# One joint transpose of the row maxima for two heads, first scores moved behind the products with v, routing in the small bank

## The chip, the cores and the metric

The kernel runs on one core of a Trainium2 chip. The metric is the device time of the whole kernel in microseconds (us). Before the change the median of three runs was 418.72 us (418.63 to 418.77). The profile comes from one more execution, which took 418.81 us.

The engines carry the names of the profile: PE multiplies matrices (PEld loads their weights), DVE is VectorE, ACT is ScalarE, POOL is GpSimd, SP issues most of the DMAs.

## What is computed

Causal attention for 8 batches of 12 heads (448 positions, 64 channels), then a soft mixture of 8 experts over all 3584 tokens, with 32 slots:

```
scores = scale * q @ k.T;  scores = where(mask, -1e9, scores)
attn = exp(scores - max(scores, -1)); attn /= sum(attn, -1) + 1e-9
x = heads side by side of attn @ v                  # 3584 x 768
logits = x @ phi                                    # 3584 x 32
d = exp(logits - logits.max(0)); d /= d.sum(0)+1e-9 # over tokens
slot_out[e] = relu((d.T @ x)[e] @ w1[e]) @ w2[e]
c = exp(logits - logits.max(1)); c /= c.sum(1)+1e-9 # over slots
return c @ slot_out
```

## The kernel before

**Pairs of heads.** The 96 heads are 48 pairs; block(p) (L507) works on pair p, with heads a = 2p and a+1. One batch is six pairs, so p % 6 says where in its batch a block stands. Every engine has an in-order queue, and a recording layer (`_InOrder`, L55) keeps the instructions in the order in which the code writes them: each queue's order is the code's order, and every row of the profile has line L65. There is no scheduler.

**Scores in two parts.** The scores of head i lie in one of three PSUM buffers, `s_[i % 3]` (each two banks of 512 columns), as blocks of keys by queries: four blocks of 128 keys with 448, 320, 192 and 64 queries. `scores1` (L249), the first scores, writes the causal mask by two bf16 matmuls (parts c03 and c12; `tri`, `identb` in the profile) and then four products k3 to k0 of rounded k and q (`s<-qd,ks`; the lower half of ks holds what rounding took from k). `max_keys` (L279) has DVE reduce this buffer by transposing 32 x 32 blocks (step 0, the large one) and folds the result by two small reductions (steps 1 and 2) into 14 columns of a tile `r`. `max_row` (L300) has PE transpose r into a small PSUM bank (`rt`) and DVE reduce it to the negated maxima `mr`. `max_spread` (L311) has POOL spread mr over rows of `r2`, next to the rest of q (`sub_q`, L243). `scores2` (L322), the second scores, adds with four matmuls both the maxima and the product with the rest of q to the buffer (`s<-r,k`). `exps` (L333) is one ACT instruction over the 1024 columns of the buffer, into `pt`.

**Products with v.** `attv` and `attv3` (L337, L351) multiply pt with v (`po<-va,pt`): 24 records for the three full query blocks of a head, and 16 for the last query block of both heads. `norm` (L368) divides by the sums, in three steps on DVE, into x. `xtrans` and `xcopy` (L386, L392) transpose x by four matmuls (`xm<-ident,x`) and copy it by ACT (`xts`).

**Routing.** `logits_a` multiplies two pairs of transposed x with phi, `logits_t` adds the result to `lt` on DVE, `logits_b` takes its maximum (`bm`, `run_m`), `logits_d` and `logits_e` make the weights of the tokens (`gs`) and transpose them and lt, `dispatch_a` multiplies them with x, and `dispatch_b` adds to `si` on DVE. Which of these a block has depends on p % 6: 1 the logits and the maximum, 2 the weights, 3 logits and a first piece of the dispatch, 4 and 0 further pieces, 5 logits. Up to p = 6 there are only logits. In the old kernel they write into the score buffer `s_[(a + 1) % 3]`, which is free at the block's end.

**PSUM.** Three score buffers (six banks), one bank po, and one small bank that `misc` (L210) hands out in turn, to rt, xm and the like: the next user waits until the last one has been read.

**Order of a block before.** PE: scores2(a), scores1(a+2), scores2(a+1), scores1(a+3), 24 products of a, rt of a+2, 24 products of a+1, 16 products, rt of a+3, the routing, xtrans(p-1). POOL: the rests of q and k for the next pairs (2 large subtractions), and two spreads, each behind its own rt. ACT: exps(a), xcopy(p-2), exps(a+1), then `copy_k2`, `cast_q` and `cast_k` for the next pairs. SP's loads of q and k stand behind the subtractions that free their buffers.

**Start and end.** Ahead of block 0 the first heads are loaded and cast by halves, and `warm` (L213) issues matmuls whose result nobody reads, START = (8, 4) of them. After block 47 come the last head's products, the last routing, the experts and the combination with the output; the change leaves that code alone.

Of the kernel before, what the change touches and what calls it, by code (L numbers as in the profile page):

```python
# [17 lines left out]
P = 128  # L18
# [7 lines left out]
NCH = 4  # L26
# [12 lines left out]
START = (8, 4)  # L39
# [9 lines left out]
RW, RC, RF = 96, 4, 20  # L49
# [31 lines left out]
def attention_soft_moe(ctx: ExitStack, tc: tile.TileContext, qk, va, phi, w1, w2, out):  # L81
# [24 lines left out]
    r_ = [fix.tile([P, RW], F32, name=f"r{i}") for i in range(2)]  # L106
# [14 lines left out]
    def load_qk(p, a, hs=slice(0, 2)):  # L121
        if p < NPAIR:
            if hs.start == 0:

                st["raw", a, p] = (wres.tile([P, 2 * WN], F32, tag="w", name=f"qk{a}_{p}")[:, 0:2 * S]
                                   .rearrange("p (h s) -> p h s", h=2)
                                   if (p, a) in ((1, 0), (2, 1)) else
                                   raw.tile([P, 2, S], F32, tag="qk", name=f"qk{a}_{p}"))
            nc.sync.dma_start(out=st["raw", a, p][:, hs], in_=qk[p, :, a, hs])
# [46 lines left out]
    load_qk(1, 1)  # L176
    load_qk(1, 0)
    loads_v(0)
    load_qk(2, 1)
    load_qk(2, 0)  # L180
    load_qk(3, 1)


# [10 lines left out]

    pob = ps_1.tile([P, 512], F32, name="po")
# [6 lines left out]
    nc.scalar.activation(out=identb, in_=ident, func=AF.Copy)  # L202
    for i in range(NR):
        nc.gpsimd.memset(r2_[i][0:64, :, :].bitcast(F32), 0.0)
        nc.vector.memset(ks_[i][:, 2 * S:2 * S + KP].bitcast(F32), 0.0)
        nc.vector.memset(r_[i], -3.0e38)
# [42 lines left out]
    def scores1(i, part):  # L249
        if i >= NHD:  # L250
            return
        p, h = divmod(i, 2)
        ks, qd = ks_[p % NR], qd_[p % NR]
        if ("s", i) not in st:
            st["s", i] = s_[i % 3]
            st["open"] = set()
        s = st["s", i]

        bank = part in ("c12", "k1", "k2")
        start = bank not in st["open"]  # L260
        st["open"].add(bank)
        if part[0] == "k":
            c = int(part[1])
            o, w, m = S * h + P * c, S - CQ0[c], min(P, S - P * c + (KP if i else 0))
            nc.tensor.matmul(s[0:m, SCOL[c]:SCOL[c] + w], ks[:, o:o + m],
                             qd[:, h, CQ0[c]:S], start=start, stop=False, skip_group_check=True)
            return
        if part == "c12":
            o = s[:, SC1:SC1 + 2 * SC2].rearrange("p (a n) -> p a n", n=SC2)[:, :, 0:P]
            mask = tri.unsqueeze(1).to_broadcast([P, 2, P])  # L270
        else:
            o, mask = s[:, SC3:SC3 + AW + P], tri2
        nc.tensor.matmul(o, identb, mask, start=start, stop=False, skip_group_check=True)

    def scores1_all(i):
        for part in ("c03", "c12", "k3", "k2", "k1", "k0"):
            scores1(i, part)

    def max_keys(i, k):  # L279

        if i >= NHD:
            return
        r = r_[i % 2]
        if k == 0:
            nc.vector.tensor_reduce(out=r[:, RC:RC + 72].rearrange("p (a b)->p a b", b=36)[:, :, 0:16],
                                    in_=st["s", i].rearrange("p (a b k)->p a b k", a=2, k=32),
                                    axis=AX.X, op=ALU.max, apply_transpose=True)  # L290
        elif k == 1:
            w = r[:, 0:84].rearrange("p (j q)->p q j", j=2)[:, 0:16]
            nc.vector.tensor_reduce(out=r[:, RF:RF + 76].rearrange("p (a q)->p a q", a=2)[:, :, 0:8],
                                    in_=w.rearrange("p (a q) j->p a q j", a=2), axis=AX.X, op=ALU.max)
        else:
            nc.vector.tensor_reduce(out=r[:, RF + 8:RF + NQB],
                                    in_=r[:, 14:80].rearrange("p (j q)->p q j", j=3)[:, 0:6],
                                    axis=AX.X, op=ALU.max)

    def max_row(i, k, w=RW - RF, to=None):  # L300
        if i >= NHD:
            return
        if k == 0:
            st["rt", i] = misc(f"rt{i}") if to is None else to
            nc.tensor.transpose(out=st["rt", i][0:w, 0:P], in_=r_[i % 2][:, RF:RF + w], identity=ident)
        else:
            mr = st["mr", i] = wk.tile([NQB, 32], F32, tag="mr", name=f"mr{i}", bufs=2)
            nc.vector.tensor_reduce(out=mr, in_=st.pop(("rt", i))[0:NQB, 0:P].rearrange("p (g t)->p t g", g=4),
                                    axis=AX.X, op=ALU.max, negate=True)

    def max_spread(i):  # L311
        if i >= NHD:
            return
        p, h = divmod(i, 2)
        mr = st.pop(("mr", i))

        nc.gpsimd.affine_select(out=r2_[p % NR][0:NQB, h].rearrange("p (b t)->p b t", t=32),
                                in_=mr.unsqueeze(1).to_broadcast([NQB, NQB, 32]),
                                compare_op=ALU.is_equal, fill=0.0, base=0,
                                pattern=[[-1, NQB], [0, 32]], channel_multiplier=1)  # L320

    def scores2(i, cs):  # L322
        if i >= NHD:
            return
        p, h = divmod(i, 2)
        s = st["s", i]
        k2, r2 = k2_, r2_[p % NR]
        for c in cs:
            o, w, m = S * h + P * c, S - CQ0[c], min(P, S - P * c + (KP if i else 0))
            nc.tensor.matmul(s[0:m, SCOL[c]:SCOL[c] + w], k2[:, o:o + m],  # L330
                             r2[:, h, CQ0[c]:S], start=False, stop=True, skip_group_check=True)
# [54 lines left out]
    def xtrans(p):  # L386
        x, xm = st.pop(("x", p)), misc(f"xm{p}")
        st["xm", p] = xm
        for c in range(NCH):
            nc.tensor.transpose(out=xm[:, P * c:P * c + P], in_=x[:, c], identity=ident)  # L390
# [58 lines left out]
    def next_logits(b, j, m):  # L449
        logits_a(b, (j, j + 1), m[:, 0:P])  # L450
        logits_t(j, m[:, 0:P])

# [32 lines left out]
    warm(START[1])  # L485
# [5 lines left out]
    nc.gpsimd.memset(si, 0.0)  # L491
    max_row(0, 0)
    max_row(0, 1)
    max_spread(0)
    scores1_all(1)
# [4 lines left out]
    sub_k(1, h1)  # L500
    for k in range(3):
        max_keys(1, k)
    sub_q(0, h1, nc.vector)
# [3 lines left out]
    def block(p):  # L507
# [10 lines left out]
        if p:  # L518
            norm(p - 1, 2)
        scores2(a, range(NCH))  # L520
        exps(a)
        if p == 0:
            copy_k2(0, h1)
            cast_q(1, h1)
        elif p > 1:
            xcopy(p - 2)
        scores1_all(a + 2)
        if p == 0:
            max_row(1, 0)
            max_row(1, 1)  # L530
            max_spread(1)
        for k in range(3):
            max_keys(a + 2, k)
        if p == 0:
            cast_k(2, h0)
# [6 lines left out]
        sub_q(p + 1)  # L542
        load_qk(p + 3, 0)
        if p:
            sub_k(p + 2)
            load_qk(p + 4, 1)
        if m6 == 2 and p > 6:
            logits_d(b, lt)
# [4 lines left out]
        if last:  # L553
            next_logits(p // 6, 2, s_[(a + 2) % 3])
# [12 lines left out]
        for h in range(2):  # L567
            attv(a + h, [(qc, 3 * h + qc, FULL) for qc in range(3)], po2, begun)
            if h == 0:
                max_row(a + 2, 0, AW)  # L570
        max_row(a + 2, 1)
        max_spread(a + 2)
        for k in (1, 2):
            max_keys(a + 3, k)
        if p == 0:
            sub_k(2, eng=nc.vector)
            load_qk(4, 1)
# [7 lines left out]
        m = s_[(a + 1) % 3]  # L585
        parts = []
        if m6 in (1, 3, 5) and p > 1:
            j = (m6 + 3) % 6
            logits_a(b if m6 == 1 else p // 6, (j, j + 1), m[:, 0:P])
        elif m6 == 2 and p > 6:  # L590
            logits_e(b, m)
        if m6 == 3 and p > 6:
            parts = [(b, 0, slice(0, P), 512)]
        elif m6 == 4 and p > 6:
            parts = [(b, 0, slice(P, 3 * P), 512)]
            if p == NPAIR - 2:
                parts += [(b, 1, slice(0, 3 * P), 0)]
        elif m6 == 0 and p > 6:
            parts = [(b - 1, 1, slice(0, 3 * P), 0)]
        for d, hf, sl, o in parts:  # L600
            dispatch_a(d, hf, m[:, o:o + sl.stop - sl.start], sl)
        if m6 in (1, 3, 5) and p > 1:
            logits_t(j, m[:, 0:P])
            if m6 == 1:
                logits_b(b, lt)
        for d, hf, sl, o in parts:
            dispatch_b(d, hf, m[:, o:o + sl.stop - sl.start], sl)
        if p:
            xtrans(p - 1)
# [319 lines left out]
```

## Time and profile before

| | value |
|---|---|
| median of three runs | 418.72 us (418.63 to 418.77) |
| profiled execution | 418.81 us, span 417.1 us, 14076 instructions |
| exponentials (pt<-s) | 96 of 1030 ns |
| large reductions on DVE (r<-s) | 96 of 1245 ns |
| transposes of maxima (rt<-ident,r) | 96 of 298 ns |
| first scores, masks included | 576 matmuls; second scores 384 |
| exponentials of head 2, and of head 94 | begin at 21.32 us and at 315.53 us |

A row of a group or of the timeline names the engine, the operation, the tiles as output<-inputs (numbers of buffers left out), shapes and a count. Starts of matmuls are recorded and their ends modelled, and matmuls overlap; so the time that PE spends on a piece of work is read here from one start to the next start. A bracket such as [1.07 <-PE s L65] tells how long the engine was idle before the instruction and what ended that. One loop turn takes about 6.4 us; the loop ends near 320 us and the experts follow.

### The profile page before, as it was taken

What the parts mean: (1) busy time and instruction counts of PE and PEld (TensorE: products, weight loads), DVE (VectorE), ACT (ScalarE), POOL (GpSimd) and SP (SyncE); (2) the same over time, 40 slices, a digit from 0 to 9 for tenths busy, and PEclk for the clock granted to TensorE, in tenths of its full rate; (3) what the DMA queues carried; (4) which work ended last, traced back from release to release, by engine and by line L of the source; (5) the groups of instructions that cost most, each with busy time, mean ns of one, the idle gap of its engine ahead of it and who ended that gap; (6) DMA issues with size and microseconds to landing.
All of it is one profiled execution on the core that took longest, in us unless ns stands there. A gap on an engine that the chain in (4) does not pass through costs nothing.

```text
span 417.1 us, 14076 instructions
## 1 busy us (share of the span) xinstructions
PE 383.6 (92%) x5710; PEld 300.0 (72%) x5710; DVE 295.2 (71%) x827; ACT 283.0 (68%) x402; POOL 263.3 (63%) x212
## 2 busy tenths in 40 slices
PE   7799999999999999999999999999998998997840
PEld 3678888888887888888888878888886644633420
DVE  6687777878877878888788778788884576433540
ACT  5677878877978888788779788887863111432430
POOL 6498898888888888988888888889862000000000
PEclk9699999999999999999999999999999999999975
DMA  7578787788777787677887777877849999999997
GB/s 275 183 228 263 251 261 224 256 260 270 236 232 243 254 283 242 224 257 247 261 270 238 230 242 255 291 236 245 278 156 415 405 426 427 421 417 415 397 394 319
DMA packets 34479, 119.16 MB, mean 286 GB/s; under 512 B 3824, under 2 KB 8944, under 8 KB 32880
## 3 DMA queue, kind: packets, MB, share of 16 engines
q1 hardware_dynamic: 34272, 118.01, 80.3%
q8 instruction: 45, 0.74, 0.7%
q10 hardware_dynamic: 144, 0.27, 0.2%
q14 instruction: 18, 0.15, 0.1%
HBM read 107.25 MB, written 11.01 MB: 284 GB/s over the span
## 4 chain that ended last, share of the span: by engine, by line
PE 78%; DVE 7%; DMA 5%; issue 3%; ACT 2%; POOL 1%; SPq 0%; DVEq 0%; POOLq 0%
PE s L65 34%; PE po L65 25%; PE xm L65 7%; PE rt L65 5%; DMA w<-in_w_dram 4%; PE so L65 2%; PE hp L65 2%; PE pp L65 2%; DVE lm L65 2%; DMA qk<-in_qk_dram 2%; DVE lg L65 1%; PE cp L65 1%; DVE r L65 1%; PE e L65 1%; DVE mr L65 1%
## 5 line engine op out<-in xcount | busy, mean ns | idle before, releaser
L65 ACT ACTIVATE pt<-s 128x1024 f32<-128x1024 f32 x96 | 98.8, 1030 | 53.5 <-PE s L65 49.9
L65 DVE TRANSPOSE_TENSOR_REDUCE r<-s 128x32 f32<-128x1024 f32 x96 | 119.5, 1245 | 20.9 <-PE s L65 18.4
L65 PE MATMUL po<-va,pt 128*64 128x65 f32 x3040 | 111.1, 226 | 0.0
L65 PEld LDWEIGHTS po<-va,pt 128*64 128x64 f32 x3040 | 97.8, 139 | 17.9 <-issue 11.9
L65 POOL TENSOR_TENSOR r<-qk,qd 64x896 fp32r<-64x896 f32 (+1 forms) x48 | 100.4, 2092 | 4.7 <-ACT qd L65 0.9
L65 POOL TENSOR_TENSOR ks<-qk,ks 64x896 fp32r<-64x896 f32 (+1 forms) x48 | 97.9, 2041 | 0.8 <-ACT ks L65 0.8
L65 POOL TENSOR_SCALAR_AFFINE_SELECT r<-mr 14x448 fp32r<-14x448 f32 x96 | 61.6, 642 | 46.2 <-DVE sm L65 26.6
L65 PE MATMUL s<-qd,ks 128*128 128x448 f32 (+4 forms) x384 | 79.8, 331 | 1.5 <-POOL ks L65 1.5
L65 PE MATMUL s<-r,k 128*128 128x448 f32 (+3 forms) x384 | 65.0, 292 | 1.4 <-POOL r L65 1.4
L65 PEld LDWEIGHTS s<-r,k 128*128 128x128 f32 (+1 forms) x384 | 59.6, 177 | 4.5 <-POOL r L65 2.3
L65 PEld LDWEIGHTS s<-qd,ks 128*128 128x128 f32 (+2 forms) x384 | 51.0, 180 | 1.7 <-POOL ks L65 1.7
L65 ACT ACTIVATE ks<-qk 128x896 fp32r<-128x896 f32 (+1 forms) x51 | 45.4, 892 | 3.7 <-DMA qk<-in_qk_dram 3.7
L65 ACT ACTIVATE qd<-qk 128x896 fp32r<-128x896 f32 (+1 forms) x50 | 46.1, 922 | 1.3
L65 ACT ACTIVATE k<-ks 64x896 fp32r<-64x896 f32 (+1 forms) x49 | 45.7, 934 | 1.1
L65 DVE TENSOR_REDUCE mr<-rt 14x32 f32<-14x128 f32 x96 | 24.8, 258 | 30.3 <-PE rt L65 30.3
L65 DVE TENSOR_REDUCE r<-r 128x16 f32<-128x32 f32 x192 | 33.7, 175 | 5.0
L65 PE MATMUL s<-tri,identb 128*128 128x192 bf16 x192 | 35.0, 264 | 0.0
L65 PE MATMUL xm<-ident,x 128*128 128x128 f32 x188 | 30.8, 286 | 3.4 <-DVE mr L65 3.4
L65 PEld LDWEIGHTS xm<-ident,x 128*128 128x128 f32 x188 | 19.7, 140 | 17.2 <-DVE sm L65 11.2
L65 PE MATMUL rt<-ident,r 128*64 128x128 f32 (+1 forms) x96 | 28.6, 298 | 1.7 <-DVE r L65 1.5
L65 ACT ACTIVATE xts<-xm 128x512 f32<-128x512 f32 x47 | 27.8, 592 | 0.2 <-PE xm L65 0.2
L65 DVE TENSOR_TENSOR x<-po,sm 128x384 f32<-128x384 f32 (+2 forms) x49 | 26.4, 540 | 0.4
(138 smaller groups left out, 355.8 us busy)
## 6 DMA issues: line engine op xcount, KB each, us to landing
qk<-in_qk_dram SPq DMA_DIRECT2D x94, 448.0 KB, 4.2
w<-in_w_dram SPq DMA_DIRECT2D x43, 768.0 KB, 7.2
w<-in_w_dram SPq DMA_DIRECT2D x10, 1536.0 KB, 20.1
va<-in_va_dram SPq DMA_DIRECT2D x47, 260.0 KB, 4.5
out_dram<-ot SPq DMA_DIRECT2D x16, 384.0 KB, 6.7
out_dram<-ot SPq DMA_DIRECT2D x2, 1536.0 KB, 9.2
qk<-in_qk_dram SPq DMA_DIRECT2D x4, 224.0 KB, 3.3
hw<-in_w_dram SPq DMA_DIRECT2D x1, 768.0 KB, 7.5
```

The costliest lines, as they stand in the source:

```text
L65: return self._tc.keep_in_program_order(op(*args, **kwargs))
```

## The change

**Maxima.** Both heads of a pair now write their folded maxima into one tile `r`, head a's from column 0 and head a+1's from column 32. One transpose `rt` per pair turns 64 columns, one DVE reduction makes mr with 46 rows, and two spreads follow each other on POOL, the second from rows 32 to 45.

**Order on PE.** scores1(a+2) stands at the head of the block, directly behind the last 16 products of the block before. Then two x transposes of pair p-2, scores2(a), two more, scores2(a+1), scores1(a+3), the routing, 24 products of a, 24 of a+1, rt of the next pair, and the 16 products.

**Routing.** It writes into the small bank amid the block. DVE's part of it comes between the large reduction of a+3 and the two small ones; ACT's copies of `logits_e` come behind exps(a+1) and ahead of `copy_k2`, and `logits_d` ahead of exps(a).

**Norm.** All three steps of the division stand at the head of the next block.

**First scores.** The parts are issued as c03, k3, c12, k2, k1, k0 instead of c03, c12, k3, k2, k1, k0; two blocks of keys of the first heads are two columns narrower.

**Start.** START = (8, 2, 2, 3), with the warming matmuls writing into po. One load of k goes through ACT's queue, loads of q and k change places, the subtractions of pairs 1 and 2 are cut by heads and partly put on DVE, and the zeroing of si moves from POOL's start to block 4.

On PE in the middle of block 15 (heads 30 and 31), before. The s_ names are the three score buffers; s_85 holds head 30 and later head 33, s_87 gets head 32, s_86 holds head 31; `r_90,k_97` or `r_98,k_97` mark second scores, `qd,ks` first scores, `tri` the mask. The four second scores of head 30 into s_85 and the first mask matmul of head 32 have just been issued:

```order
L65 MATMUL s_87<-tri_129,identb 128x2x128
L65 MATMUL s_87<-qd_88,ks_89 66x64
L65 MATMUL s_87<-qd_88,ks_89 128x192
L65 MATMUL s_87<-qd_88,ks_89 128x320
L65 MATMUL s_87<-qd_88,ks_89 128x448
L65 MATMUL s_86<-r_98,k_97 128x448
L65 MATMUL s_86<-r_98,k_97 128x320
L65 MATMUL s_86<-r_98,k_97 128x192
L65 MATMUL s_86<-r_98,k_97 66x64
L65 LDWEIGHTS identb
L65 MATMUL s_85<-tri_129,identb 128x192
```

The same place after the change, from the second scores of head 30:

```order
L65 MATMUL s_85<-r_97,k_96 128x448
L65 MATMUL s_85<-r_97,k_96 128x320
L65 MATMUL s_85<-r_97,k_96 128x192
L65 MATMUL s_85<-r_97,k_96 66x64
L65 MATMUL xm_1673<-ident,x_94 128x128 x2
L65 MATMUL s_86<-r_97,k_96 128x448
L65 MATMUL s_86<-r_97,k_96 128x320
L65 MATMUL s_86<-r_97,k_96 128x192
L65 MATMUL s_86<-r_97,k_96 66x64
L65 LDWEIGHTS identb
L65 MATMUL s_85<-tri_117,identb 128x192
```

Between the last second score of s_85 and the mask that starts head 33 in s_85 there were six matmuls of head 32 and four of head 31; now there are two x transposes and the four of head 31.

On PE at the end of block 15, before: behind the second rt follow two pairs' logits, a dispatch piece, the x transposes and the second scores of the next block.

```order
L65 MATMUL rt_1796<-ident,r_96 64x128
L65 MATMUL s_86<-xts_1622,phi_153 32x128 x4
L65 MATMUL s_86<-xts_1725,phi_153 32x128 x4
L65 MATMUL s_86<-x_103,gs 32x128 x4
L65 MATMUL xm_1818<-ident,x_94 128x128 x4
L65 MATMUL s_87<-r_90,k_97 128x448
```

After the change, from the last first score of head 33 to the only rt of the block (twelve of these matmuls with v are 24 records of the trace):

```order
L65 MATMUL s_85<-qd_88,ks_89 128x448
L65 MATMUL m_1706<-xts_1587,phi_151 32x128 x4
L65 MATMUL m_1706<-xts_1683,phi_151 32x128 x4
L65 MATMUL m_1706<-x_102,gs 32x128 x4
L65 MATMUL po<-va_99,pt_98 64x65 x12
L65 MATMUL po<-va_99,pt_100 64x65 x12
L65 MATMUL rt_1750<-ident,r 64x128
```

The routing has moved ahead of the products with v, into the bank `m`, and rt stands once, behind both heads' 24 products.

On DVE at the end of block 13 (p % 6 = 1), before: the large reduction of the second head, then its small ones, each mr behind its rt, and the routing (lt, bm, run_m) last.

```order
L65 TENSOR_REDUCE r_96<-s_87 128x2x16
L65 TENSOR_REDUCE mr_1575<-rt_1561 14x32
L65 TENSOR_REDUCE r_96<-r_96 128x2x8
L65 TENSOR_REDUCE r_96<-r_96 128x6
L65 TENSOR_REDUCE mr_1590<-rt_1588 14x32
L65 TENSOR_SCALAR sm_1593<-po 128x7
L65 RECIPROCAL sm_1593<-sm_1593 128x7
L65 TENSOR_TENSOR lt<-s_85,lt 128x128
L65 TENSOR_REDUCE bm_1605<-lt 128x1
L65 TENSOR_SCALAR run_m_156<-run_m_155,bm_1605 128x1
```

And after:

```order
L65 TENSOR_REDUCE r<-s_87 128x2x16
L65 TENSOR_TENSOR lt<-m_1504,lt 128x128
L65 TENSOR_REDUCE bm_1514<-lt 128x1
L65 TENSOR_SCALAR run_m_154<-run_m_153,bm_1514 128x1
L65 TENSOR_REDUCE r<-r 128x2x8
L65 TENSOR_REDUCE r<-r 128x6
L65 TENSOR_REDUCE mr_1548<-rt_1546 46x32
L65 TENSOR_SCALAR sm_1571<-po 128x7
```

The three routing instructions now stand ahead of the two small reductions on which rt waits.

The diff, cut to its core:

```diff
-START = (8, 4)
+START = (8, 2, 2, 3)
...
-    r_ = [fix.tile([P, RW], F32, name=f"r{i}") for i in range(2)]
+    r_ = fix.tile([P, RW], F32, name="r")
...
     def scores1_all(i):
-        for part in ("c03", "c12", "k3", "k2", "k1", "k0"):
+        for part in ("c03", "k3", "c12", "k2", "k1", "k0"):
...
-    def max_row(i, k, w=RW - RF, to=None):
-        if i >= NHD:
+    def max_row(p, k):
+        if p >= NPAIR:
             return
         if k == 0:
-            st["rt", i] = misc(f"rt{i}") if to is None else to
-            nc.tensor.transpose(out=st["rt", i][0:w, 0:P], in_=r_[i % 2][:, RF:RF + w], identity=ident)
+            st["rt", p] = misc(f"rt{p}")
+            nc.tensor.transpose(out=st["rt", p][0:AW, 0:P], in_=r_[:, 0:AW], identity=ident)
...
-        if p:
-            norm(p - 1, 2)
-        scores2(a, range(NCH))
-        exps(a)
+        if m6 == 2 and p > 6:
+            logits_d(b, lt)
         if p == 0:
...
-        elif p > 1:
-            xcopy(p - 2)
-        scores1_all(a + 2)
...
+        else:
+            scores1_all(a + 2)
+            for k in range(3):
+                norm(p - 1, k)
+            if p > 1:
+                xtrans(p - 2, range(2))
+            scores2(a, range(NCH))
+            exps(a)
+            if p > 1:
+                xtrans(p - 2, range(2, NCH))
+                xcopy(p - 2)
         for k in range(3):
             max_keys(a + 2, k)
+        if p == 4:
+            nc.gpsimd.memset(si, 0.0)
         scores2(a + 1, range(NCH))
         exps(a + 1)
...
         scores1_all(a + 3)
         max_keys(a + 3, 0)
...
+        parts = []
         if m6 == 2 and p > 6:
-            logits_d(b, lt)
+            logits_e(b, misc(f"le{p}"))
+        elif m6 in (1, 3, 5) and p > 1 or m6 in (0, 4) and p > 6:
+            m, j = misc(f"m{p}"), (m6 + 3) % 6
...
+            for d, hf, c0, c1, o in parts:
+                dispatch_a(d, hf, m[:, o:o + c1 - c0], slice(c0, c1))
+            if m6 % 2:
+                logits_t(j, m[:, 0:P])
+                if m6 == 1:
+                    logits_b(b, lt)
+            for d, hf, c0, c1, o in parts:
+                dispatch_b(d, hf, m[:, o:o + c1 - c0], slice(c0, c1))
+        for k in (1, 2):
+            max_keys(a + 3, k)
         copy_k2(p + 1)
...
         for h in range(2):
             attv(a + h, [(qc, 3 * h + qc, FULL) for qc in range(3)], po2, begun)
-            if h == 0:
-                max_row(a + 2, 0, AW)
-        max_row(a + 2, 1)
-        max_spread(a + 2)
-        for k in (1, 2):
-            max_keys(a + 3, k)
+        max_row(p + 1, 0)
+        max_row(p + 1, 1)
+        for h in range(2):
+            max_spread(p + 1, h)
...
         attv3(p)
-        max_row(a + 3, 0, AW)
-        max_row(a + 3, 1)
-        max_spread(a + 3)
-        for k in range(2):
-            norm(p, k)
...
-        if p:
-            xtrans(p - 1)
```

More of the change, by code (lines that the diff above doesn't have):

```diff
@@ L313, in max_spread @@
             return
[L314 to L318, printed above, removed]
+        mr, r = st["mr", p], slice(32 * h, 32 * h + NQB)
+        nc.gpsimd.affine_select(out=r2_[p % NR][r, h].rearrange("p (b t)->p b t", t=32),
+                                in_=mr[r].unsqueeze(1).to_broadcast([NQB, NQB, 32]),
                                 compare_op=ALU.is_equal, fill=0.0, base=0,
@@ L384, in norm, with xtrans @@
                                         scalar1=sm[a:a + AW, 2 * m:2 * m + 1], scalar2=None, op0=ALU.mult)
[L386 to L389, printed above, removed]
+    def xtrans(p, cs=range(NCH)):
+        if cs[0] == 0:
+            st["xm", p] = misc(f"xm{p}")
+        x, xm = st["x", p], st["xm", p]
+        for c in cs:
             nc.tensor.transpose(out=xm[:, P * c:P * c + P], in_=x[:, c], identity=ident)
@@ L568, in block @@
             attv(a + h, [(qc, 3 * h + qc, FULL) for qc in range(3)], po2, begun)
-            if h == 0:
-                max_row(a + 2, 0, AW)
-        max_row(a + 2, 1)
-        max_spread(a + 2)
-        for k in (1, 2):
-            max_keys(a + 3, k)
+        max_row(p + 1, 0)
+        max_row(p + 1, 1)
+        for h in range(2):
+            max_spread(p + 1, h)
         if p == 0:
-            sub_k(2, eng=nc.vector)
-            load_qk(4, 1)
+            sub_k(2, h1)
         attv3(p)
-        max_row(a + 3, 0, AW)
-        max_row(a + 3, 1)
-        max_spread(a + 3)
-        for k in range(2):
-            norm(p, k)
[L585 to L607, printed above, removed]
-        if p:
-            xtrans(p - 1)
     for p in range(NPAIR):
```

95 lines of the change are left out of this document (53 added, 42 removed).

## The prediction

> **What bounds it.** I read first the busy times (of the page, and of a long stretch of the loop over pairs), then the chain piece by piece, then the timeline of one block. The first says which engine is short, the second what a block costs, the third what is waited for within it.
>
> ```profile
> PE 383.6 (92%) x5710; PEld 300.0 (72%) x5710; DVE 295.2 (71%) x827; ACT 283.0 (68%) x402; POOL 263.3 (63%) x212
> 60.00:300.00 240.00, 238.36 (x3868) 202.03 (x3867) 194.48 (x539) 201.58 (x266) 205.70 (x151) 1.00 0.77 252
> ```
>
> The second row gives PE, PEld, DVE, ACT and POOL in turn, for 240 us of the loop, some 38 blocks. PE has holes of 1.6 us in all; POOL, ACT and DVE have 34, 38 and 46 us, so 0.9 to 1.2 us in each block. Whatever PE issues here is paid for, and so is whatever makes it stand.
>
> ```profile
> 103.97 2.52 PE s L65 x20
> ...
> 110.22 2.58 PE s L65 x20
> ...
> 116.81 2.52 PE s L65 x20
> 119.33 0.85 PE po L65 x24
> 120.17 0.23 PE rt L65
> 120.41 1.32 PE po L65 x40
> 121.72 0.23 PE rt L65
> 121.95 0.57 PE s L65 x8
> 122.52 0.59 PE xm L65 x4
> 123.11 2.51 PE s L65 x20
> ...
> 129.40 2.52 PE s L65 x20
> ...
> 135.91 2.51 PE s L65 x20
> ...
> 142.21 2.52 PE s L65 x20
> ```
>
> These are pieces of the chain (start, us, what). A block reads: twenty score matmuls, products with v of head a (po x24), a transpose of maxima (rt), the other products (po x40), the second rt, a routing piece (the short "s"), the x transposes (xm). From one "x20" to the next are the periods of blocks 14 to 19, one batch of six: 6.25, 6.59, 6.30, 6.29, 6.51, 6.30, together 38.24 us.
>
> **The window that decides.** Block 17 in the timeline:
>
> ```profile
> 122.45 0.66 PE L65 MATMUL xm<-ident,x 128*128 128x128 f32 x4
> 122.86 0.71 PE L65 MATMUL s<-r,k 128*128 128x448 f32 x4
> 123.42 0.36 PE L65 MATMUL s<-tri,identb 128*128 128x192 bf16 x2
> 123.61 1.03 ACT L65 ACTIVATE pt<-s 128x1024 f32<-128x1024 f32 x1 [1.07 <-PE s L65]
> 124.19 0.63 PE L65 MATMUL s<-r,k 128*128 128x448 f32 x4
> 124.39 1.25 DVE L65 TRANSPOSE_TENSOR_REDUCE r<-s 128x32 f32<-128x1024 f32 x1 [0.30 <-PE s L65]
> 124.69 0.35 PE L65 MATMUL s<-tri,identb 128*128 128x192 bf16 x2
> 124.80 0.82 PE L65 MATMUL s<-qd,ks 128*66 128x64 f32 x4
> 125.55 0.86 PE L65 MATMUL po<-va,pt 128*64 128x65 f32 x22
> 125.68 0.40 DVE L65 TENSOR_REDUCE r<-r 128x16 f32<-128x32 f32 x2
> ```
>
> By starts: second scores of a at 122.86, first scores of a+2 at 123.42 (0.56 later), second scores of a+1 at 124.19 (0.77), first scores of a+3 at 124.69 (0.50), products with v at 125.55 (0.86). There are three score buffers, so head a+3 writes the one that held head a. Its first matmul must wait for the exponentials of head a: these run from 123.61 to 124.64, and it starts at 124.69. So 1.83 us lie between the second scores of a and the first scores of a+3 whatever PE does between, and the old order has just that much to do there: 0.56 + 0.77 + 0.50.
>
> **The change in the loop.** It takes the first scores of a+2 (0.77) out of this window and puts them ahead of it. In their place comes half of the x transposes; all four take 122.86 − 122.45 = 0.41, so half 0.20. PE reaches head a+3 after 0.56 + 0.20 + 0.50 = 1.26 and stands for 1.83 − 1.26 = 0.57 us. Behind it are queued the scores, the routing and all products with v, and DVE's maxima wait for those scores. The exponentials cannot start earlier, since ACT already waits for PE there (idle 1.07). One of the two transposes of maxima goes (0.23).
>
> A new block by starts: first scores 0.77, half of x 0.20, window 1.83, first scores 0.86, routing M, 48 products 0.85 + 24/40 × 1.32 = 1.64, a wait W for the maxima, rt 0.23, the last 16 products 0.53. That is 6.06 + M + W. The old one was 2.69 + 0.85 + 0.23 + 1.32 + 0.23 + 0.41 = 5.73 + M. So each block gains **0.33 + W**. M is the old period less 5.73, thus 0.57 in blocks 16, 17, 19, 0.86 in block 15, 0.78 in block 18. Block 14 is other: it has only two transposes as routing (0.20, as above), and its old period hides a wait of the x transposes for the small bank, 0.3; the new order ends that.
>
> W is there because the one rt now needs the maxima of both heads. I count from the second scores of a. The first scores of a+3 end at 124.80 + 0.82, so at 2.76. The large reduction follows 0.03 later, as at 124.39; with its 1.25 and the two small ones rt may start at 4.51. PE gets there at 1.83 + 0.86 + 1.64 = 4.33 + M. But DVE's part of the routing now stands between the large reduction and the small ones:
>
> ```profile
> L65 DVE SCALAR_TENSOR_TENSOR si<-si,al,s 128x384 f32<-128x384 f32 x7 | 4.3, 614 | 1.3 <-PE s L65 1.3
> L65 DVE TENSOR_TENSOR lt<-s,lt 128x128 f32<-128x128 f32 x14 | 4.1, 292 | 1.3 <-PE s L65 1.1
> L65 DVE SCALAR_TENSOR_TENSOR si<-si,al,s 128x256 f32<-128x256 f32 x7 | 3.4, 481 | 0.7 <-PE s L65 0.7
> L65 DVE SCALAR_TENSOR_TENSOR si<-si,al,s 128x128 f32<-128x128 f32 x7 | 2.4, 339 | 0.0
> L65 DVE TENSOR_REDUCE bm<-lt 128x1 f32<-128x128 f32 x7 | 2.0, 286 | 0.2
> L65 DVE TENSOR_SCALAR run_m<-run_m,bm 128x1 f32<-128x1 f32 x7 | 1.5, 214 | 0.3
> ```
>
> With 0.03 between two of them, p % 6 = 1 (block 19) adds lt, bm and run_m, 0.88: ready at 5.39 where PE is there at 4.90, W = 0.49. Block 16 adds 256 columns, 0.51: 5.02 against 4.90, W = 0.12. Block 15 adds lt and 128 columns, 0.69: 5.20 against 5.19, W = 0.01. Block 18 adds 384 columns, 0.64: 5.15 against 5.11, W = 0.04. Blocks 17 and 14 have 0 and, at 4.33 + 0.20, 0. The changes of blocks 14 to 19 are then +0.01, +0.34, +0.45, +0.33, +0.37 and +0.82: **+2.32 us per batch**. Routing runs with all its parts from block 7; up to block 45 that is six batches and three blocks (p % 6 = 1, 2, 3, together 1.17), so 6 × 2.32 + 1.17 = **+15.1 us**.
>
> **The other engines.** POOL's work stays, but its two spreads now follow each other behind rt.
>
> ```profile
> L65 POOL TENSOR_TENSOR r<-qk,qd 64x896 fp32r<-64x896 f32 x40 | 84.5, 2114 | 3.2
> L65 POOL TENSOR_TENSOR ks<-qk,ks 64x896 fp32r<-64x896 f32 x39 | 81.9, 2101 | 0.0
> L65 POOL TENSOR_SCALAR_AFFINE_SELECT r<-mr 14x448 fp32r<-14x448 f32 x80 | 51.3, 642 | 35.7 <-DVE sm L65 22.3 <-DVE mr L65 13.2
> ```
>
> 2.11 + 2.10 + 2 × 0.64 = 5.5 us fits in 6.3. Behind the start of rt I estimate 0.4 to the reduction mr, 0.3 for it and 0.7 with the hand-over for the first spread, 1.4 in all. PE asks for it after 0.23 + 0.53 + 0.77 + 0.20 = 1.73, so 0.3 us of cover is left; were it gone, each 0.1 us late costs 4 us in 40 blocks. ACT keeps its order but for the routing's copies, which come before its casts in p % 6 = 2; its 1.0 us of holes cover them. The loads of q and k are issued behind the same subtractions as before, and a longer block only gives them more time. Writing the first scores as c03, k3, c12 issues the same matmuls; another order of weight loads may win or lose 0.05 in each of 92 sets, ±4.6 us. I take 0, as the window's rows show them back to back.
>
> **Start and end.** Blocks 1 to 6 lack most of the routing. Those without any stood before as block 14 does, and are like it now: no change, and ±1.5 for the logits and the first waits. The start has another order of loads and subtractions, no zeroing of si on POOL, and more warming matmuls.
>
> ```profile
> 13.19:20.02 6.83, 5.96 (x63) 5.12 (x65) 4.11 (x9) 4.38 (x6) 3.37 (x3) 0.50 0.39 138
> ```
>
> Here the granted clock was 0.50, with PE busy for 5.96 us. At full clock this would be half, so at most −3.0; what PE waits for from POOL and DVE stays, and a lost overlap may cost +0.5. I take **−1.0**. At the end, the spreads ahead of the last pair have no first scores to hide behind (+0.5), and in block 47 the last x transposes wait for DVE's sum of the logits in the same bank, one lt of 0.29: **+0.8**.
>
> [...]
>
> **The sum.** 15.1 + 0 − 1.0 + 0.8 = +14.9. The profiled execution took 418.81 us (span 417.1), 0.09 over the median of 418.72. So 433.7, and I say **434**.
>
> **Rivals.** First: PE waits nowhere anew, and the saved transpose counts. That needs the exponentials to free the buffer 1.26 us after the second scores begin, not 1.83; from about 1.5 on the block gains. Then 47 × 0.23 = 10.8 us go, and some 408 are left. For it speaks that the old trace lists no wait of PE there; against it, that the matmul of head a+3 starts just 0.05 us behind the exponentials' end. Chance 0.08.
>
> Second: the exponentials do bind, but the weight loads win their 4.6 us, the start its 3.0 (2.0 more than I took), and W is half of mine (−2.2): 434 − 9 = 425. All three at once or still more: 418 to 427, chance 0.12, of which 0.02 within 0.2% of the old time.
>
> Third: the cover of 0.3 us behind rt is too thin. If mr or the spread is 0.2 to 0.4 later than that, the second scores wait for POOL too in every block: +8 to +16, so 442 to 450. For it speaks that rt, mr, spread and second scores are now one chain with little beside it; against it, that POOL has 0.8 us to spare in a block and DVE nothing queued ahead of mr. Chance 0.10.
>
> That the order is not what the change says I give nothing: its rows show the moves.
>
> **How the numbers follow.** My own case, 427 to 441, has 0.70. The range for 8 in 10 runs from 424, the second rival's ends together, to 443, the third's lower end. A measurement of this kernel tells 0.2%, 0.8 us, from no change. Faster 0.08, within 0.2% 0.02, slower 0.90.
>
> **What would show it.** Right: in a block of the new profile the first mask matmul of a+3 waits some 0.5 us for ACT pt and starts 1.8 us behind the second scores of a; rt waits for DVE r, longest where p % 6 = 1; there is one rt per block; periods are 6.3 to 7.1. Wrong: no wait of PE for ACT; a wait of the second scores for POOL (third rival); first scores well under 0.77; a start that differs by over 3 us.

## The result, and the profile after

The changed kernel takes **428.57 us** (median of 4 runs, 428.09 to 429.06), the one before 418.75 us in the same session (4 runs, 418.63 to 419.34). The ratio is 1.0232, with a 95% interval of 1.0214 to 1.025: slower, by 9.8 us. Forecast were 434 us and a range of 424 to 443. The profiled execution took 428.09 us, its span is 426.4 us (417.1 before).

The busy times of the page, and below them the same stretch of the loop as before:

```profile
PE 371.3 (87%) x5674; PEld 287.2 (67%) x5674; DVE 294.9 (69%) x779; ACT 283.6 (67%) x402; POOL 265.6 (62%) x215
60.00:300.00 240.00, 221.06 (x3678) 185.31 (x3668) 187.52 (x481) 193.89 (x254) 196.83 (x145) 1.00 0.74 240
```

PE had 1.6 us of holes in 240 us, and now has 18.9. It issues fewer instructions, and stands more. For whom it stands, the list of PE's waits from 60 to 310 us tells (us in total, times, longest; first before, then after):

```profile
PE xm L65 <- DVE mr L65: 1.6, 7, 0.2
PE rt L65 <- DVE r L65: 0.3, 1, 0.3
```

```profile
PE s L65 <- ACT pt L65: 14.5, 37, 0.4
PE rt L65 <- DVE r L65: 4.2, 14, 0.4
PE s L65 <- ACT qd L65: 1.1, 7, 0.2
```

Two waits are new: for the exponentials (once a block) and for ACT's cast of q (once in six blocks). The wait of the x transposes for the small bank is gone. The wait of rt for the maxima, once in the old list, now comes in 14 blocks. Block 17 in the timeline, in the order of the starts:

```profile
123.73 0.72 PE L65 MATMUL s<-r,k 128*128 128x448 f32 x4
124.28 0.41 PE L65 MATMUL xm<-ident,x 128*128 128x128 f32 x2
124.45 0.71 PE L65 MATMUL s<-r,k 128*128 128x448 f32 x4
124.48 1.03 ACT L65 ACTIVATE pt<-s 128x1024 f32<-128x1024 f32 x1 [1.31 <-PE s L65]
124.51 1.25 DVE L65 TRANSPOSE_TENSOR_REDUCE r<-s 128x32 f32<-128x1024 f32 x1
125.56 0.24 PE L65 MATMUL s<-tri,identb 128*128 128x192 bf16 x1 [0.40 <-ACT pt L65]
...
126.93 1.62 PE L65 MATMUL po<-va,pt 128*64 128x65 f32 x48
...
128.48 0.30 PE L65 MATMUL rt<-ident,r 128*64 128x128 f32 x1
```

From the second scores of a (123.73) to the first mask of a+3 (125.56) there are 1.83 us, to the hundredth what the window had before. PE has 0.55 + 0.17 for the first two pieces by their starts, and some 0.55 for the third like the first: 1.27. So it stands for **0.56 us**. The bracket says only 0.40, as it counts from the modelled end of the matmul before; for a stand behind matmuls, take starts. ACT shows that nothing is late on its side: it starts 0.75 behind the first second score, runs 1.03, and PE goes on 0.05 behind it. Here rt waits for nothing: it comes 1.55 behind the start of the 48 products. So block 17, 6.30 us long before and 6.45 now, has 5.89 us of work and 0.56 of standing: the change took 0.41 us of work out of it and put more standing in.

Where the 9.3 us of span went, by the starts of exponentials in both traces (of heads 2, 14, 92 and 94; before first, then after):

```profile
21.32 1.02 ACT L65 ACTIVATE pt<-s 128x1024 f32<-128x1024 f32 x1 [1.73 <-PE s L65]
59.63 1.03 ACT L65 ACTIVATE pt<-s 128x1024 f32<-128x1024 f32 x1 [1.02 <-PE s L65]
308.55 1.03 ACT L65 ACTIVATE pt<-s 128x1024 f32<-128x1024 f32 x1 [2.24 <-PE s L65]
315.53 1.03 ACT L65 ACTIVATE pt<-s 128x1024 f32<-128x1024 f32 x1 [3.58 <-issue]
```

```profile
19.31 1.02 ACT L65 ACTIVATE pt<-s 128x1024 f32<-128x1024 f32 x1 [0.61 <-PE s L65]
57.84 1.02 ACT L65 ACTIVATE pt<-s 128x1024 f32<-128x1024 f32 x1 [1.06 <-PE s L65]
317.62 1.02 ACT L65 ACTIVATE pt<-s 128x1024 f32<-128x1024 f32 x1 [2.54 <-DVE x L65]
324.37 1.03 ACT L65 ACTIVATE pt<-s 128x1024 f32<-128x1024 f32 x1 [3.35 <-issue]
```

| stretch | before | after | difference | forecast |
|---|---|---|---|---|
| start, up to head 2 | 21.32 | 19.31 | −2.0 | −1.0 |
| blocks 1 to 6 | 38.31 | 38.53 | +0.2 | 0 |
| **loop**, blocks 7 to 45 | 248.92 | 259.78 | +10.9 | +15.1 |
| block 46 and the end | 6.98 + 101.57 | 6.75 + 102.03 | +0.2 | +0.8 |
| sum | 417.1 | 426.4 | +9.3 | +14.9 |

"Loop" below always means this stretch, from head 14 to head 92.

### The profile page after: what moved, and what is told of

It is laid out like the page before. It is cut to its first block, busy times and chain, and to the rows that moved or that the text cites. A ratio compares the mean times of both kernels' runs of the same rounds, so it can differ in the third digit from the quotient of the medians.

```text
span 426.4 us, 13855 instructions
## 1 busy us (share of the span) xinstructions
PE 371.3 (87%) x5674; PEld 287.2 (67%) x5674; DVE 294.9 (69%) x779; ACT 283.6 (67%) x402; POOL 265.6 (62%) x215
## 5 line engine op out<-in xcount | busy, mean ns | idle before, releaser
L65 PE MATMUL po<-va,pt 128*64 128x65 f32 x3040 | 109.8, 225 | 0.0
L65 POOL TENSOR_TENSOR ks<-qk,ks 64x896 fp32r<-64x896 f32 (+1 forms) x49 | 99.3, 2026 | 0.7 <-ACT ks L65 0.5
L65 PE MATMUL s<-r,k 128*128 128x448 f32 (+3 forms) x384 | 68.7, 301 | 1.8 <-POOL r L65 1.8
L65 PEld LDWEIGHTS s<-qd,ks 128*128 128x128 f32 (+2 forms) x384 | 52.3, 183 | 26.2 <-issue 22.8
L65 PEld LDWEIGHTS s<-r,k 128*128 128x128 f32 (+1 forms) x384 | 56.1, 176 | 4.6 <-POOL r L65 3.0
L65 PE MATMUL s<-tri,identb 128*128 128x192 bf16 x192 | 40.5, 269 | 18.1 <-ACT pt L65 18.1
L65 PE MATMUL xm<-ident,x 128*128 128x128 f32 x188 | 37.2, 280 | 0.4 <-DVE lt L65 0.4
L65 DVE TENSOR_REDUCE mr<-rt 46x32 f32<-46x128 f32 x49 | 13.8, 282 | 28.4 <-PE rt L65 28.4
L65 DVE TENSOR_SCALAR x<-po,sm 64x64 f32<-64x64 f32 x94 | 26.2, 278 | 0.7
L65 PEld LDWEIGHTS xm<-ident,x 128*128 128x128 f32 x188 | 22.6, 141 | 3.6 <-DVE lt L65 0.7
```

The costliest lines, as they stand in the source:

```text
L65: return self._tc.keep_in_program_order(op(*args, **kwargs))
```

## The experiments

All are edits of the kernel after, unless the text names the one before. The numbers in short; the last two columns (loop, and the start of head 2's exponentials) come from the profiled execution:

| run | median us (lowest to highest) | ratio to before, 95% | loop | head 2 starts |
|---|---|---|---|---|
| before | 418.75 (418.63 to 419.34) | | 248.9 | 21.32 |
| after | 428.57 (428.09 to 429.06) | 1.0232 (1.0214 to 1.025) | 259.8 | 19.31 |
| a_oldorder | 432.38 (431.71 to 433.1) | 1.0323 (1.0295 to 1.0351) | 263.5 | 20.21 |
| b_neworder | 415.19 (414.74 to 416.02) | 0.9914 (0.9887 to 0.9942) | 246.5 | 20.92 |
| a_window | 430.37 (429.33 to 431.28) | 1.0274 (1.024 to 1.0308) | 260.7 | 21.25 |
| a_window_x4 | 430.21 (429.48 to 431.08) | 1.0265 (1.0232 to 1.0298) | 260.6 | 21.36 |
| a_half_exp | 409.59 (409.46 to 409.7) | 0.9794 (0.9769 to 0.9818) | 242.7 | 19.35 |
| a_late_max | 425.06 (424.87 to 427.07) | 1.0171 (1.0145 to 1.0197) | 256.5 | 21.73 |
| a_cast_first | 425.76 (425.52 to 427.31) | 1.0189 (1.0166 to 1.0213) | 257.4 | 19.54 |
| a_cold | 430.85 (429.99 to 431.98) | 1.0301 (1.0276 to 1.0325) | 259.7 | 23.15 |
| a_x4_nosmall | 420.24 (419.98 to 420.61) | 1.0037 (1.0023 to 1.005) | 252.5 | 19.29 |
| a_fix | 422.91 (422.51 to 424.23) | 1.0109 (1.009 to 1.0129) | 254.1 | 19.94 |
| b_neworder_warm | 414.22 (414.07 to 415.94) | 0.9901 (0.9884 to 0.9918) | 246.4 | 19.47 |

The start varies by up to 2.4 us between kernels that have the same code there, and its granted clock with it: from 6.80 to 13.60 us the mean is 0.59 in a_late_max (head 2 at 21.73) and 1.00 in after (19.31). So the loop of the profiled execution is the better measure of an edit in the loop.

**The window, by its length: a_half_exp.**

```diff
-  activation(out=pt_[i % 2][:, 0:1024], in_=st.pop(("s", i)), func=AF.Exp, scale=SCALE)
+  activation(out=pt_[i % 2][:, 512:1024], in_=st.pop(("s", i))[:, 512:1024], func=AF.Exp, scale=SCALE)
```

The other half of `pt` is zeroed once at the start, so half of the attention weights are left out.

> The changed kernel with the exponentials taken over one bank of the scores only (columns 512 to 1023); the other half of pt is set to zero once at the start and never filled, so half of the attention weights are left out. It prices the wait for the exponentials by itself: the instruction should take about 0.60 us, as the copy xts of 512 columns does. Theory (PE stands for the exponentials of a in each block): the window shrinks from 1.83 to some 1.40 us, PE waits 0.13 there, the block loses 0.33 to 0.43 us, 408 to 413 us. Rival (the two earlier runs with the first scores put back gained nothing, so something else sets the block, such as DVE's two large reductions in a row): the wait moves to rt <- DVE r and the time stays within 425 to 429 us.

It took 409.59 us, 19.0 less. The same place of a block:

```profile
118.21 0.72 PE L65 MATMUL s<-r,k 128*128 128x448 f32 x4
...
118.94 0.71 PE L65 MATMUL s<-r,k 128*128 128x448 f32 x4
118.97 0.60 ACT L65 ACTIVATE pt<-s 128x512 f32<-128x512 f32 x1 [1.74 <-PE s L65]
119.62 0.24 PE L65 MATMUL s<-tri,identb 128*128 128x192 bf16 x1
```

The exponential is 0.43 us shorter, the window 0.42 (1.41 in place of 1.83), and the blocks are 0.42 to 0.48 shorter (the loop 17.1 us, 39 blocks). The first mask again starts 0.05 behind the exponential's end (118.97 + 0.60). So that end sets the window, and what is taken out of it is gained in full in each block. In this run no matmul was taken away, and the wait of rt for the maxima is as in after (4.2 us, 14 times).

**The window, by its contents: a_window and a_window_x4.** The first scores of a+2 go back into the window; in a_window_x4 all four x transposes stand ahead of it too, as in the old kernel. The rest of the change stays.

```diff
-  scores1_all(a + 2)      # head of the block
   ...
-  xtrans(p - 2, range(2))
+  xtrans(p - 2)           # a_window_x4 alone
   scores2(a)
   exps(a)
+  scores1_all(a + 2)
-  xtrans(p - 2, range(2, NCH))   # a_window_x4 alone
```

> The changed kernel, with the first scores of a+2 put back between the second scores of a and of a+1; half of the x transposes stays ahead of the window, half in it. Joint transpose, routing in the small bank and the new order of parts stay. Theory (the missing 0.71 us in the window is the cause): no wait for the exponentials is left, as the window now holds 0.55 + 0.71 + 0.17 + 0.52 = 1.95 us of work; but the spread of the maxima loses its cover (asked for 0.23 + 0.62 + 0.14 = 0.99 us behind rt, ready at 1.46), so PE waits 0.47 us for POOL r in each block. Block 5.75 + M + W instead of 5.87 + M + W, some -5 us, 424 us. Rival (joint transpose or routing in the small bank cause the loss): 428.5 us or more, with waits elsewhere.

> As the run before, but all four x transposes stand ahead of the second scores of a, so that they cover the spread. Theory: the spread is asked for 0.23 + 0.62 + 0.41 = 1.26 us behind rt, so PE waits 0.2 us for POOL r; the window holds 0.55 + 0.71 + 0.50 = 1.76, so 0.07 us for ACT pt; block 5.63 + M + W, -0.24 x 39 = -9 us, 419 us. Rival (the window is not the cause): 428.5 us or more.

Both missed, by 6 and by 11 us: 430.37 and 430.21. In the profiled executions the later start (head 2 at 21.25 and 21.36) accounts for 2 us; the loops, 260.7 and 260.6, are no shorter than that of after, 259.8. The waits of a_window_x4 from 60 to 310 us:

```profile
PE rt L65 <- DVE r L65: 14.8, 37, 0.8
PEld s L65 <- POOL r L65: 7.2, 37, 0.2
```

The wait for the exponentials has left the list, as expected. In its place PE waits for the maxima in each block (14.8 us, 4.2 in after), and for POOL's spread. The timeline of block 16 shows how:

```profile
119.71 0.74 PE L65 MATMUL s<-r,k 128*128 128x448 f32 x4
120.29 0.26 PE L65 MATMUL s<-tri,identb 128*128 128x192 bf16 x1
...
121.28 1.25 DVE L65 TRANSPOSE_TENSOR_REDUCE r<-s 128x32 f32<-128x1024 f32 x1 [0.58 <-PE s L65]
121.57 0.24 PE L65 MATMUL s<-tri,identb 128*128 128x192 bf16 x1
...
122.56 0.40 DVE L65 TENSOR_REDUCE r<-r 128x16 f32<-128x32 f32 x2
122.88 1.24 DVE L65 TRANSPOSE_TENSOR_REDUCE r<-s 128x32 f32<-128x1024 f32 x1
124.04 0.44 DVE L65 SCALAR_TENSOR_TENSOR si<-si,al,m 128x256 f32<-128x256 f32 x1
124.40 0.39 DVE L65 TENSOR_REDUCE r<-r 128x16 f32<-128x32 f32 x2
124.93 0.27 PE L65 MATMUL rt<-ident,r 128*64 128x128 f32 x1 [0.39 <-DVE r L65]
```

DVE can start on head a+2 only at 121.28, 1.57 behind the second scores of a; in after it starts 0.78 behind them (124.51 against 123.73), since the scores stand at the block's head. From there two large reductions, a routing piece and the small reductions follow each other without a gap, and the one rt needs both heads' maxima. In the old kernel the first rt needed only the first head's.

By starts, rt comes 1.80 to 2.37 us behind the start of the products in blocks 14 to 19 of a_window_x4, where 1.55 is the products' own time: it stands 2.75 us in the batch, in after 0.89. That is 0.31 more in a block, and eats the 0.24 that was forecast as gain. In a_window PE stands 0.47 for the spread, as expected (0.61 from the x transposes to the second scores in place of 0.14), but rt stands 1.89 us in the batch. My expectation had counted PE's side alone.

**Is it DVE's queue? a_x4_nosmall.** a_window_x4, where DVE drops the two small reductions of head a+2 from block 1 on.

```diff
-  for k in range(3):
+  for k in range(1 if p else 3):
       max_keys(a + 2, k)
```

> The run a_window_x4 without the two small reductions of head a+2 from block 1 on, so that the maxima of one head of each pair are left stale. Theory (with the first scores put back, both large reductions follow each other behind them and DVE's chain makes rt late: 19.4 us of waiting ahead of rt in all, 6.7 in the changed kernel): 0.39 us less on DVE ahead of rt takes 0.25 to 0.39 us out of each wait, 2.1 us in a batch, -14 us, 416 us. Rival (rt is late for another reason, the bank or the products with v): 430 us.

It took 420.24 us, 4 more than expected; the loop went from 260.6 to 252.5, by 0.2 a block. The direction bears the reading out. The size is short of the expected: in block 16 the second large reduction starts 1.26 behind the first (116.30 and 117.56) in place of 1.60, so 0.34 earlier, but only with p % 6 = 2, where no routing piece stands behind it on DVE, does rt gain that much (0.32). In the other blocks the routing piece starts 1.28 behind the second large reduction (118.84) in place of 1.16, the small ones 0.04 later still, and rt gains 0.17 to 0.18. Why that is so stays open. The run is no proposal; it only tells what rt waits for.

**The maxima in p % 6 = 1: a_late_max.** Block 19 in after, where DVE's routing stands between the large reduction and the small ones:

```profile
139.66 1.25 DVE L65 TRANSPOSE_TENSOR_REDUCE r<-s 128x32 f32<-128x1024 f32 x1 [0.34 <-PE s L65]
140.06 1.62 PE L65 MATMUL po<-va,pt 128*64 128x65 f32 x48
140.83 0.25 DVE L65 TENSOR_TENSOR lt<-m,lt 128x128 f32<-128x128 f32 x1
141.12 0.28 DVE L65 TENSOR_REDUCE bm<-lt 128x1 f32<-128x128 f32 x1
141.44 0.21 DVE L65 TENSOR_SCALAR run_m<-run_m,bm 128x1 f32<-128x1 f32 x1
141.57 0.39 DVE L65 TENSOR_REDUCE r<-r 128x16 f32<-128x32 f32 x2
142.10 0.27 PE L65 MATMUL rt<-ident,r 128*64 128x128 f32 x1 [0.43 <-DVE r L65]
```

In block 17 rt came 1.55 behind the start of the products; here it is 2.04, so 0.49 late. The edit puts bm and run_m behind the reduction mr:

```diff
-  if m6 == 1:
-      logits_b(b, lt)     # behind lt
   ...
   max_row(p + 1, 1)
+  if m6 == 1 and p > 1:
+      logits_b(b, lt)
```

> The changed kernel with the maximum of the logits (bm, run_m on DVE, p % 6 = 1) made behind the reduction mr instead of ahead of the two small reductions of a+3. Theory (these two instructions make rt wait 0.50 us in one block of six): the wait goes in 7 blocks, -3.5 us; 0.1 to 0.2 us of it come back in the block after, since the division and the next large reduction start later; 425 to 426.2 us. Rival (the wait is hidden behind something else): 428.5 us.

425.06 us; the block went from 6.92 to 6.45, the loop by −3.3, and rt comes 1.55 behind the start of the products again.

**The cast of q in p % 6 = 2: a_cast_first.** The end of block 14 in after:

```profile
106.72 1.62 PE L65 MATMUL po<-va,pt 128*64 128x65 f32 x48
...
108.50 0.27 PE L65 MATMUL rt<-ident,r 128*64 128x128 f32 x1 [0.17 <-DVE r L65]
108.65 0.95 ACT L65 ACTIVATE qd<-qk 128x896 fp32r<-128x896 f32 x1
109.32 0.26 PE L65 MATMUL s<-tri,identb 128*128 128x192 bf16 x1
109.74 0.22 PE L65 MATMUL s<-qd,ks 128*66 128x64 f32 x1 [0.16 <-ACT qd L65]
```

Elsewhere the first product starts 0.04 behind its mask; here it takes 0.42, and the cast ends at 109.60. Ahead of the cast stand the three ACT instructions of logits_e (two copies and the update of run_z, from 106.93) and the cast of k. The edit:

```diff
   def logits_e(b, tp, p):
       ...
+      cast_q(p + 2)      # ahead of the three ACT instructions
   ...
-  cast_q(p + 2)
+  if not (m6 == 2 and p > 6):
+      cast_q(p + 2)
```

> The changed kernel with the cast of the next q put ahead of the three copies of the routing on ACT in blocks with p % 6 = 2. Theory (there the first scores of the next block wait 0.36 us for ACT qd): 7 x 0.36 = -2.5 us, 426 us; the copies then come later, and rt, which needs their bank, may wait 0.1 for them. Rival (the copies only change places with the cast, and rt waits as long): 428.5 us.

425.76 us; block 14 went from 6.65 to 6.29, the loop by −2.4, and the wait for qd is gone from the list.

**Both: a_fix.**

> a_late_max and a_cast_first together in the changed kernel. Theory (the two waits stand in different blocks, so they add): 428.5 - 3.5 - 2.8 = 422.2 us. Rival (one hides the other): 425 us.

422.91 us; the loop is 5.7 shorter, as the two together (3.3 + 2.4). Still 1.0109 (1.009 to 1.0129) of the time before.

**The order of the first scores: a_oldorder and b_neworder.** The new order of parts taken out of the new kernel, and put into the old one:

```diff
-  for part in ("c03", "k3", "c12", "k2", "k1", "k0"):
+  for part in ("c03", "c12", "k3", "k2", "k1", "k0"):   # b_neworder: the other way round
```

> The changed kernel, with the first scores issued again as c03, c12, k3, k2, k1, k0. Theory (the new order of the six matmuls is what made the changed block 0.13 us shorter than I had it: 0.71 and 0.79 us where the old order takes 0.78 and 0.86): both sets lie outside the pinned window now, so the block becomes 0.13 us longer, 46 x 0.13 = +6 us, 434.5 us; the wait for the exponentials stays at 0.56. Rival (the order of the parts costs nothing, and the block was mis-sized elsewhere): 428.5 us.

> The kernel before, with the first scores issued as c03, k3, c12, k2, k1, k0 and nothing else. Theory (1.83 us from the second scores of a to the first scores of a+3 are pinned by the exponentials): the gain in the set that lies inside this window is eaten by a wait of some 0.05 us for them, only the other set gains 0.07, so about -3 us, 415.5 us, and PE waits for ACT pt appear. Rival one (PE is bound by its own work, both sets count): -6 us, 412.7 us. Rival two (the order costs nothing): 418.7 us.

After with the old order takes 432.38 us, 3.8 more; the first scores take 0.78 and 0.86 by starts in place of 0.71 and 0.79, and most blocks are 0.11 to 0.13 longer. The expected 434.5 was missed by 2: with p % 6 = 2 the block is 0.04 shorter (6.61), since both masks now go ahead of the first product and cover a part of its wait for qd (by starts 0.24 is left of 0.38). The old kernel with the new order takes 415.19 us, as expected, a ratio of 0.9914 (0.9887 to 0.9942). Its window:

```profile
121.98 0.71 PE L65 MATMUL s<-r,k 128*128 128x448 f32 x4
122.54 0.26 PE L65 MATMUL s<-tri,identb 128*128 128x192 bf16 x1
...
122.73 1.03 ACT L65 ACTIVATE pt<-s 128x1024 f32<-128x1024 f32 x1 [1.01 <-PE s L65]
...
123.25 0.63 PE L65 MATMUL s<-r,k 128*128 128x448 f32 x4
...
123.71 0.10 PEld L65 LDWEIGHTS <-identb 128*128 128x128 bf16 x1
123.81 0.24 PE L65 MATMUL s<-tri,identb 128*128 128x192 bf16 x1
```

Still 1.83, though the first scores in it take 0.71 (122.54 to 123.25). What the order saves within the window is lost there: the mask's weights are loaded at 123.71, and the mask starts 0.10 later, 0.05 behind the end of the exponentials (122.73 + 1.03); before, it started 0.03 behind the load (124.66 and 124.69). The expected wait for pt is not in the list of PE's waits; only the starts show it. The set behind the window counts: most blocks are 0.06 shorter (with p % 6 = 2 by nothing, with 3 by 0.11), the loop 2.4. So the old window was full and pinned at the same time, as the prediction had it.

**The start: a_cold and b_neworder_warm.** a_cold takes the five warming matmuls that the change added later in the start away, START = (8, 2, 0, 0); b_neworder_warm adds five to b_neworder.

```diff
   scores1_all(1)
+  warm(2, pob)
   ...
+  warm(3, pob)
   max_row(1, 0)
```

> The changed kernel with START = (8, 2, 0, 0): without the two groups of warming matmuls in the start, five in all. [...] Rival (the other order of loads and subtractions gains the 2 us at the start): 428 to 428.5 us.

> b_neworder with two groups of warming matmuls added in the start, two behind the first scores of head 1 and three behind those of head 2, as in the changed kernel; two transposes and the routing place of the kernel before. Theory (the warming matmuls keep the clock at 1.00 from 13 to 20 us, and that gains 1 to 2 us at the start): 413 to 414 us, faster than both kernels. Rival (the start of the kernel before waits for POOL and DVE, and the clock does not matter): 415.2 us.

Busy times and granted clock (the third number from the right) in the start of after, a_cold and b_neworder_warm:

```profile
13.19:20.02 6.83, 5.88 (x89) 5.16 (x90) 5.38 (x13) 5.17 (x7) 5.85 (x7) 1.00 0.48 145
```

```profile
13.60:20.40 6.80, 5.26 (x51) 4.17 (x51) 4.13 (x8) 5.02 (x8) 4.37 (x4) 0.50 0.40 138
```

```profile
13.19:20.02 6.83, 5.62 (x88) 4.46 (x86) 5.57 (x13) 4.68 (x6) 3.89 (x4) 1.00 0.44 147
```

Without the five matmuls the stretch has a granted clock of 0.50, head 2 starts 3.8 us later in the profiled execution, and the median is 2.3 us higher (430.85, above the 428 to 428.5 of the rival). The mean granted clock of the whole span is 0.972 to 0.977 in the five executions of a_cold, and 0.982 to 0.984 in the four of after. Five such matmuls are no guarantee: a_window has them too, and two of its four executions have 0.975; in its profiled one the stretch from 13.19 to 20.02 us has 0.85. In the old kernel with the new order, five such matmuls go with a clock of 1.00, and head 2 starts at 19.47 in place of 20.92. The time, 414.22 us, is the lowest of the runs that compute everything, and 1% below before (0.9901, 0.9884 to 0.9918), but its interval overlaps that of b_neworder: the two are not told apart in total time.

## Why the prediction was right, and where its terms were off

**The stand for the exponentials was right**, in place, cause and size: 1.83 pinned, 0.57 forecast, 0.56 by starts. a_half_exp shows that it sets the block, and b_neworder that the old window was bound to the same 1.83. The first rival (nothing waits, some 408) needed a release at 1.26.

**W was right where DVE's routing makes it**: 0.49 (0.49 forecast) for p % 6 = 1, 0.12 (0.12) in block 16, 0.05 (0.04) in block 18, 0 in blocks 15 and 17. a_late_max takes the first away. For p % 6 = 2 I forecast 0 and it is 0.23: rt starts at 108.50, 1.78 behind the start of the products. By the step's own sum PE was there only 0.02 later than the maxima; the shorter first scores and products (1.55, not 1.64) brought it there earlier, and PE starts 0.14 behind the reductions' end.

**The step that failed is "I take 0" for the order of the first scores**, by size: it was worth 0.06 and 0.07 a set, as a_oldorder shows by itself. Together with the half of the x transposes ahead of the window at 0.14 in place of 0.20, a block is 5.87 + M + W and not 6.06. In the 32 blocks of the loop with p % 6 other than 2 that is −6.1 us. The bound given, 0.05 either way, had no row behind it and was also too tight.

**"ACT's 1.0 us of holes cover them" was wrong.** The busy time did not say when the holes come. In p % 6 = 2 the copies stand between the exponentials and the cast of q, and the first scores, now at the head of the block, ask for that cast 0.38 us before they can go on. With W this made block 14 longer by 0.4 (6.26 to 6.65) where +0.01 was forecast: seven such blocks in the stretch, 2.7 us. a_cast_first shows the mechanism by itself. The two errors partly cancel, which is luck: 15.1 − 6.1 + 2.7 is 11.7, measured 10.9; the remaining 0.8 is not traced.

**Start and end.** The start gained 2.0, not 1.0, within its bounds. The clock was 1.00 in place of 0.50, which a_cold undoes; there head 2 starts at 23.15, later than the 21.32 of before, so in these executions the gain comes with the clock and not from the other edits of the start. In the three rows above the clock is 1.00 with the added matmuls (after, b_neworder_warm) and 0.50 without them (a_cold), while a_window has them and 0.85. The −3.0 that the prediction gave as the most was my estimate (half of the 5.96 us that PE was busy at 0.50) and was not reached. The end cost 0.2 and not 0.8: block 46 became 0.2 shorter, and the rest 0.5 longer.

**The second rival** was near: the order of the weight loads and a part of the start came as it has them, but W came out higher and not at half, and the cast of q was a wait more. **The third** (the spread late) did not occur in after: POOL is not in PE's list of waits. It does occur in a_window and a_window_x4, where PE asks for the spread earlier. Of the signs named, the waits for pt and r, the one rt per block and the periods (6.45 to 6.92) came; so did one of the wrong ones, first scores under 0.77 (0.71), which is the mis-sized term above.

**What stays open.** That the two halves of the change need each other is shown from one side: with the first scores back in the window, rt waits for DVE instead. The joint transpose alone in the old kernel, with the routing where it was, was not tried; nor was an exponential in two pieces with a buffer freed by banks; whether the first scores then wait for the first piece alone, no run shows. Why DVE's routing piece follows a large reduction later in a_x4_nosmall, and why the order of the first scores matters, no run tells.

## What to carry to other kernels

Here the work between the reading and the overwriting of a buffer covered the reader's latency (1.83 us from the second scores of a to the first mask of a+3): before moving such work out, add up by starts what is left there (1.27 in after), and expect to pay the difference (0.56) in every turn of the loop. One wait for two results in place of two waits saved an instruction (0.23 us) but bound rt to the later result (it stood 0.89 us in a batch of after, 2.75 in one of a_window_x4), so the producer's queue had to be free at that point; look at what stands between in that queue, not at the engine's share of busy time. Edits of a few lines beside the large change (the order of six matmuls, −2.4 us of loop in the old kernel) can be worth having without it.

## What was not expected of the hardware

The order of six short matmuls that each load weights mattered: mask, product, mask, products takes 0.71 and 0.79 us by starts in after where mask, mask, products takes 0.78 and 0.86 in a_oldorder, with the same instructions and no wait in either. And the start's clock hung on little: five matmuls whose result nobody reads make the difference between a_cold (0.50 from 13.60 to 20.40 us) and after (1.00). PE busy for 5.96 of 6.83 us had 0.50 before, 5.88 had 1.00 after. Busy time can't tell the two apart, since the matmuls of before took longer at 0.50: 24 products with v take 1.50 us by starts there (from 16.68 us), and 0.85 at 1.00 (from 125.55). Before, 63 matmul records filled that stretch, after 89.
